# Token pairs 2 and 3 of an SSD scan: B and C in 512-byte rows, turned on VectorE

## Chip, cores and metric

One Trainium2 chip, one core, everything in float32 to the outside. The metric is the device time of one execution in microseconds (us); lower is better. Time before: 355.99 us, the median of three runs (355.82, 355.99, 357.87).

## The reference, cut to what matters

Two blocks follow each other. The first is a Mamba-2 scan in chunks of 32 tokens over x (4 batches, 8 heads, 768 tokens, 32 channels) with B and C (16 states a head) and decays a; the second is a feed-forward block with a learned slope on its negative side.

```python
for c in range(nc):                                   # chunks of 32 tokens
    cum = np.cumsum(la, axis=-1)                      # la: log of the clipped a
    L = np.exp(cum[:, :, :, None] - cum[:, :, None, :]) * causal
    CB = np.einsum('bhin,bhjn->bhij', Cc, Bc)         # contracts over the 16 states
    y_intra = np.einsum('bhij,bhjd->bhid', CB * L, xc)
    y_inter = np.einsum('bhin,bhnd->bhid', Cc, state) * exp(cum)
    state = decay_full * state + sum_j(B_j x_j decay_from_j)   # contracts over tokens
...
h = x @ w_in                                          # 3072 x 256 by 256 x 2048
g = np.maximum(h, 0.0) + alpha * np.minimum(h, 0.0)
out = g @ w_out                                       # 2048 x 256
```

What matters here: B is needed twice, with tokens on the partitions (for the state) and with states on the partitions (for C times B). C is needed with states on the partitions alone. In memory both lie as [batch, head, token, state], so one token of one head is 16 numbers, 64 bytes.

## The kernel before

**Tiling.** The kernel works in chunks of 128 tokens, two chunks (256 tokens) to a "pair", numbered gp = 0 to 11; with 768 tokens a batch has three pairs. Two pairs make a group g of 512 tokens, and the feed-forward block runs by groups. Pairs 0 and 1 are done first by `first_two`, with code of their own. Pairs 2 and 3 run between the feed-forward steps of group 0. From pair 4 on (`fine = gp >= 4`) the stages of `pair` are cut finer and lie between the steps of `quad`, the feed-forward code of groups 1 to 5.

**Order.** There is no scheduler: the order of instructions on each engine is the order of the program, written out by hand. `pair` is a generator; each `ssm(gp)` runs it to its next `yield`. The loop for group 0 goes over f = 4 to 15: `hidden(0, f)` (TensorE, line L1095, then ScalarE L1098 and VectorE L1099), a stage of `ssm(2)` for f up to 10 and of `ssm(3)` from f = 9, the conversion of weight pieces, and `output(f - 4)` (TensorE L1142). So the first stage of pair 2 comes behind `hidden(0, 4)` and that of pair 3 behind `hidden(0, 9)`.

**Weights.** w_in and w_out arrive as 64-bit floats in 16 pieces of 512 KB each, alternating between the two, with rows of 2 KB (`load_weights`, L257, tile `raw`). Each piece is converted by ScalarE (L273, then L283 or L286), VectorE (L296, L308) and GpSimd (L278 clamps, L330 adds); only then can TensorE use it. Below, in4 is the fifth piece of w_in, out1 and out2 the second and third of w_out.

**Loads of a pair.** `load_pair(gp)` issues all on SP's queue. `load_bc(k)` (L192) brings B and C of chunk k into `nat`, tokens on the partitions, in 1024 runs of 64 bytes each; `load_x(k)` (L197) brings x in runs of 128 bytes. For pair 2 `load_pair(2, False, True)` issues chunk 0 only; the two closures it returns are called a little later in `first_two`, between weight pieces. For pair 3 all is issued at f = 5. For pairs above 4 (`turned`), C is not loaded by `load_bc`; instead both B and C are also loaded in four transfers of 128 rows of 512 bytes (L215): 8 tokens of one head lie in one row, even heads and odd heads apart. Transfers of one queue are issued in the order of the program.

**To states on the partitions.** For pairs 2, 3 and 4, `pair` does four TensorE transposes of 128x128 into a PSUM tile (L669) and one ScalarE copy of 128x512 out of it (L672), giving `bc`. For pairs from 5 on, `turn_bc(gp)` does one VectorE instruction (L574) from the 512-byte rows. After that come `spread_c` (ScalarE, L679), `c_decayed` (GpSimd, L682), the C times B products (TensorE, L742), their product with the decays (VectorE, L753) and the products with x (TensorE, L797, L805). `pair_loads` makes `bn` from B with tokens on the partitions (GpSimd, L533); TensorE multiplies it with x at L629. The scans that make the decays are VectorE's, L567 for pairs 2 and 3. `token_sums` is four subtractions on GpSimd (L1183) ahead of the products of a group (TensorE, L1241).

**PSUM.** `ss_tile()` deals tiles in turn from a rotation: two tiles of the pool `ps_s` and one bank of `ps_q`. The transposes of pairs 2 and 3 take one tile each of it.

Of the kernel before, what the change touches and what calls it, by code (L numbers as in the profile page):

```python
# [9 lines left out]
F32 = mybir.dt.float32  # L10
# [12 lines left out]
def kernel(  # L23
# [25 lines left out]
    nc = tc.nc  # L49
# [5 lines left out]
    N = B.shape[-1]  # L55
    P = 128
    Q = 128
# [8 lines left out]
    GC = 4  # L66
# [9 lines left out]
    NB = 2  # L76
# [15 lines left out]
    work = ctx.enter_context(tc.tile_pool(name="work", bufs=2))  # L92
# [4 lines left out]
    gp = ctx.enter_context(tc.tile_pool(name="gp", bufs=16))  # L97
# [15 lines left out]
    def ss_tile():  # L113
        if early[0] is None:
            return ps_s.tile([P, 512], F32, name="ss")
        early[0] += 1
        i = early[0] % (3 if ident_p else 4)
        return ps_s.tile([P, 512], F32, name="ss") if i < 2 else bank(i)


    loads = {}

    def load_rows(i, eng=nc.sync):

        rows = ld.tile([RW, Q], F32, name="rows")
        eng.dma_start(out=rows, in_=a.rearrange("b h (c t) -> (b h c) t", t=Q)[i * RW : (i + 1) * RW])
        loads["r", i] = rows
# [3 lines left out]
    def load_a(t, b, c, eng=nc.sync):  # L131
        first = a[b, 0:1, c * Q : (c + 2) * Q]
        eng.dma_start(out=t, in_=bass.AP(tensor=first.tensor, offset=first.offset,
                                             ap=[[S, H], [0, N], [1, 2 * Q]]))
# [4 lines left out]
    def load_tokens(dst, src, t0):  # L139


        d = dst.rearrange("p j (h w) -> p j h w", h=H)
        for k in range(2):
            for j in range(2):
                t = t0 + k * Q + j * HQ
                nc.sync.dma_start(out=d[HQ * k : HQ * (k + 1), j],
                                  in_=src[:, t : t + HQ, :].rearrange("h p w -> p h w"))

    def load_spread(gp, b, c):

        for w, t in enumerate(loads["p", gp][1] if gp >= HALF else ()):
            rows = scratch["z", b // 2].rearrange("(b h c) t -> b c h t", b=2, h=H)
            for k in range(2):
                nc.sync.dma_start(
                    out=t[HQ * k : HQ * (k + 1), : 4 * SQ].rearrange("p (h t) -> p h t", h=4),
                    in_=rows[b % 2, c + k, 4 * w : 4 * w + 4].unsqueeze(0)
                    .to_broadcast([HQ, 4, SQ]))
        for k, t in enumerate(loads["p", gp][1] if gp < HALF else ()):
            rows = scratch["z", b // 2].rearrange("(b h c) t -> b c h t", b=2, h=H)[b % 2, c + k]
            nc.sync.dma_start(out=t.rearrange("p (h t) -> p h t", h=H),  # L160
                              in_=rows.unsqueeze(0).to_broadcast([P, H, Q]))
            yield

    def load_products(gp, ap):
        b, c = divmod(2 * gp, CPB)
        rows = scratch["pf", b // 2].rearrange("(b h c) t -> b h (c t)", b=2, h=H)
        rows = rows[b % 2, :, c * Q : (c + 2) * Q]
        nc.sync.dma_start(out=ap, in_=rows.unsqueeze(1).to_broadcast([H, N, 2 * Q]))

    def load_pair(gp, decays=True, parted=False):  # L170


        b, c = divmod(2 * gp, CPB)
        turned = gp > GC
        nat = ldx.tile([P, 3, 2, H * N], F32, name="nat")
        xt = ldx.tile([P, 2, HD], F32, name="xt")

        ap = ldx.tile([P, 2 * Q], F32, name="ap")
        if gp == 0:
            load_a(ap, b, c)  # L180
        elif gp > NB:
            load_products(gp, ap)
        if gp == 0:
            load_rows(0, nc.scalar)
        abc = []
        if gp >= HALF:
            load_tokens(nat[:, 0], B[b], c * Q)
        def load_bc(k):
            ts = slice((c + k) * Q, (c + k + 1) * Q)
            for i, src in enumerate((B,) if turned else (B, C)):  # L190
                eng = nc.scalar if gp == 0 and i else nc.sync
                eng.dma_start(out=nat[:, i, k].rearrange("p (h n) -> p h n", h=H),  # L192
                              in_=src[b, :, ts, :].rearrange("h p n -> p h n"))

        def load_x(k):
            ts = slice((c + k) * Q, (c + k + 1) * Q)
            nc.sync.dma_start(out=xt[:, k].rearrange("p (h d) -> p h d", h=H),  # L197
                              in_=x[b, :, ts, :].rearrange("h p d -> p h d"))

        for k in range((1 if parted else 2) if gp < HALF else 0):  # L200
            load_bc(k)
            if gp >= NB:
                load_x(k)
        for k in range(2 if gp < NB else 0):
            load_x(k)
        if gp == 0:
            nc.scalar.dma_start(out=al_n, in_=moe_alpha.rearrange("(k p) -> k p", p=P))
            loads["a", 1] = prep.tile([P, 2 * Q], F32, name="a1")
            load_a(loads["a", 1], b, c + 2)
        for i, src in enumerate((B, C) if turned else ()):  # L210


            for e in range(2):
                first = src[b, e : e + 1, c * Q : (c + 2) * Q, :]
                nc.sync.dma_start(out=nat[:, 1 + e, i],  # L215
                                  in_=bass.AP(tensor=first.tensor, offset=first.offset,
                                              ap=[[2 * S * N, P // 32], [8 * N, 32], [1, 8 * N]]))
        for k in range(2 if gp >= NB else 0):
            abc.append(lda.tile([P, H * Q], F32, name="abc"))
        loads["p", gp] = nat, abc, xt, ap  # L220
        if gp >= HALF:
            load_tokens(xt, x[b], c * Q)
        if decays:
            for part in load_spread(gp, b, c):
                pass
        return lambda: load_bc(1), lambda: load_x(1)
# [6 lines left out]

    al_n = const.tile([NF, P], F32, name="al_n")
    load_pair(0)

    w_in = const.tile([P, KC, d_ff], F32, name="w_in")
# [312 lines left out]
    bcs = {}  # L550
# [3 lines left out]
    def scan_half(dec, abc, k, w):  # L554
        dv = dec.rearrange("p k h t -> p k (h t)")
        if ident_p and halved:
            dv = dec.rearrange("p k h t -> p (k h t)")
            for i in range(2):
                s = (2 * w + i) * SQ
                o = (4 * k + 2 * w + i) * SQ  # L560
                nc.vector.tensor_tensor_scan(out=dv[:, o : o + SQ], data0=abc[k][:, s : s + SQ],  # L561
                                             data1=ident_p[0][:, :SQ], initial=0.0,
                                             op0=ALU.mult, op1=ALU.add)
            return
        for i in range(2):
            hs = slice((2 * w + i) * 2 * Q, (2 * w + i + 1) * 2 * Q)
            nc.vector.tensor_tensor_scan(out=dv[:, k, hs], data0=abc[k][:, hs],  # L567
                                         data1=ident_p[0], initial=0.0, op0=ALU.mult,
                                         op1=ALU.add)

    def turn_bc(gp):

        bcs[gp] = work.tile([P, 4, Q], F32, name="bc")
        nc.vector.transpose(  # L574
            bcs[gp].rearrange("p (i k) t -> p i (k t)", i=2)
            .rearrange("p i (c b) -> p i b c", b=8),
            loads["p", gp][0][:, 1:].rearrange("p e i (b n) -> p (i b) e n", n=N))
        decs[gp] = work.tile([P, 2, H, Q], F32, name="dec")
        scan_half(decs[gp], loads["p", gp][1], 0, 0)

    def pair(gp):

        b, c = divmod(2 * gp, CPB)
        nat, abc, xt, ap = loads["p", gp]
        last = c + 2 == CPB
        fine = gp >= 2 * GC // 2
# [75 lines left out]


        bc = bcs.pop(gp, None)
        if bc is None:
            tp = ss_tile()
            for i in range(2):
                for k in range(2):
                    nc.tensor.transpose(tp[:, (2 * i + k) * P : (2 * i + k + 1) * P],  # L669
                                        nat[:, i, k], ident)  # L670
            bc = work.tile([P, 4, Q], F32, name="bc")
            nc.scalar.copy(out=bc.rearrange("p i t -> p (i t)"), in_=tp)  # L672
# [148 lines left out]
    def first_two():  # L821
# [158 lines left out]
        prq = rows_short(rq)  # L980
        rows_out(0)
        load_pair(1)
        load_second()
        nat1, _, xt1, pf1 = loads["p", 1]
# [420 lines left out]
    def ssm(gp, stages=1):  # L1405

        if gp not in pairs:
            pairs[gp] = pair(gp)
        for i in range(stages):
            next(pairs[gp], None)  # L1410
# [169 lines left out]
```

## Time and profile before

| | us |
|---|---|
| median of three runs | 355.99 |
| span of the profiled execution, first to last instruction | 355.9 |
| TensorE busy (matmul) | 349.3 |
| VectorE, GpSimd, ScalarE busy | 235.8, 204.4, 171.8 |
| share of the DMA engines, 18 to 27, 27 to 36, 36 to 45 us | 0.92, 0.95, 0.96 |
| TensorE clock granted | 1.000 |

For the profiled execution no time beside its span is given; the span lies 0.1 us under the median of the runs, so next to nothing lies around it. Busy time of TensorE counts a matmul from its start to its modelled end; matmuls overlap, so the step from one start to the next is the better measure of what one costs. Names like L1142 are lines of the kernel before; an arrow reads "out <- in". Of the changed kernel, lines from 578 on lie 5 to 7 lower.

### The profile page before, as it was taken

The numbers are of one execution on the slowest core, as the hardware profiler recorded it, in microseconds if no ns is written. First come the engines' busy times: TensorE is split into PE (matmuls) and PEld (weight loads), VectorE is DVE, ScalarE is ACT, GpSimd is POOL, SyncE is SP. The second block draws the span as 40 slices with busy tenths as digits, with TensorE's granted clock in tenths as the row PEclk, the third lists the DMA queues.
The fourth block names the chain that finished last, engine by engine and source line by source line (L and its number), as shares of the span: only waits on it lengthen the run. The fifth ranks groups of instructions, "written<-read, shape, count | busy, mean of one in ns | idle before, by whom it ended". The sixth has DMA issues, their size and how long they took to land.

```text
span 355.9 us, 7778 instructions
## 1 busy us (share of the span) xinstructions
PE 349.3 (98%) x2985; PEld 284.4 (80%) x2985; DVE 235.8 (66%) x482; ACT 171.8 (48%) x391; POOL 204.4 (57%) x228
## 2 busy tenths in 40 slices
PE   8899999999999999999999999999999999999996
PEld 4576665578788888888888888888888888888885
DVE  6876986998748756847747856757856633643363
ACT  3477576535355346345345445345445344443431
POOL 6776568589939855725646626637526535434520
PEclk9999999999999999999999999999999999999999
DMA  7899989607345403503423423422001001001102
GB/s 138 182 202 270 329 174 279 148 17 159 106 83 128 102 3 75 104 2 77 78 57 74 86 51 71 85 55 65 11 2 31 0 2 29 2 1 31 31 0 59
DMA packets 105581, 30.24 MB, mean 85 GB/s; under 512 B 79896, under 2 KB 101448, under 8 KB 105544
## 3 DMA queue, kind: packets, MB, share of 16 engines
q1 hardware_dynamic: 103048, 29.43, 36.3%
q10 hardware_dynamic: 2496, 0.32, 0.6%
q8 instruction: 23, 0.38, 0.5%
q14 instruction: 14, 0.11, 0.1%
HBM read 26.32 MB, written 3.42 MB: 84 GB/s over the span
## 4 chain that ended last, share of the span: by engine, by line
PE 89%; SPq 4%; DMA 3%; DVE 2%; ACT 1%; POOL 1%; issue 0%; DVEq 0%; ACTq 0%
PE bank L1216 33%; PE hp L1241 29%; PE bank L1142 6%; PE ss L1241 6%; PE hp L1095 3%; DMA raw<-in_moe_w_in_dram 2%; SPq L192 2%; PE ss L787 1%; PE ss L731 1%; PE hp L1110 1%; PE bank L1209 1%; PE ss L805 1%; PE ss L779 1%; DMA xt<-in_x_dram 1%; SPq L197 1%; PE ss L742 1%
## 5 line engine op out<-in xcount | busy, mean ns | idle before, releaser
L1298 POOL TENSOR_TENSOR gt<-gt 128x512 f32<-128x512 f32 x58 | 74.2, 1279 | 21.1 <-DVE gt L1226 16.3
L1216 PE MATMUL bank<-gt,w_out 128*128 128x256 f32 x320 | 83.5, 381 | 0.0
L1216 PEld LDWEIGHTS bank<-gt,w_out 128*128 128x128 f32 x320 | 60.1, 190 | 9.2 <-issue 1.0
L1288 POOL TENSOR_TENSOR gt<-gt 128x512 f32<-128x512 f32 x20 | 25.4, 1269 | 62.5 <-DVE gt L1226 49.7
L1226 DVE SCALAR_TENSOR_TENSOR gt<-hp,s_mul,gt 128x256 f32<-128x256 f32 x96 | 42.0, 479 | 29.1 <-ACT gt L1224 26.8
L1224 ACT ACTIVATE gt<-hp,s_alpha 128x256 f32<-128x256 f32 x96 | 40.3, 471 | 34.5 <-PE hp L1241 31.4
L1216 PE MATMUL bank<-gt,ws 128*128 128x256 f32 x224 | 55.9, 379 | 0.0
L1216 PEld LDWEIGHTS bank<-gt,ws 128*128 128x128 f32 x224 | 42.3, 190 | 5.6
L1241 PE MATMUL hp<-xs,w_in 128*128 128x256 f32 x160 | 41.9, 384 | 0.0
L1241 PE MATMUL hp<-xs,ws 128*128 128x256 f32 x160 | 41.1, 380 | 0.0
L1267 DVE TENSOR_TENSOR hp<-hp,u 128x512 f32<-128x512 f32 x20 | 14.0, 700 | 35.2 <-ACT u L1265 35.2
L1241 PEld LDWEIGHTS hp<-xs,ws 128*128 128x128 f32 x160 | 30.3, 190 | 4.3 <-POOL xs L1183 0.2
L1241 PEld LDWEIGHTS hp<-xs,w_in 128*128 128x128 f32 x160 | 29.7, 190 | 4.5
L1142 PE MATMUL bank<-w_out,gt 128*128 128x256 f32 x128 | 31.1, 385 | 0.4 <-POOL w_out L330 0.4
L1142 PEld LDWEIGHTS bank<-w_out,gt 128*128 128x128 f32 x128 | 23.6, 190 | 7.2 <-issue 2.9
L1241 PE MATMUL ss<-xT,w_in 128*128 128x256 f32 x96 | 24.6, 379 | 0.0
L645 POOL TENSOR_TENSOR sm<-state,bmask 128x256 f32<-128x256 f32 (+1 forms) x10 | 6.2, 620 | 29.0 <-DVE state L642 29.0
L1095 PE MATMUL hp<-xT,w_in 128*128 128x512 f32 x48 | 22.8, 596 | 0.0
L561 DVE TENSOR_TENSOR_SCAN dec<-abc,bank 128x192 f32<-128x192 f32 x48 | 22.7, 522 | 0.0
L1256 ACT COPY m<-hp 128x512 f32<-128x512 f32 x8 | 4.7, 586 | 35.7 <-PE hp L1241 35.7
L1265 ACT COPY u<-hp 128x512 f32<-128x512 f32 x20 | 11.7, 585 | 19.4 <-PE hp L1241 19.4
L1226 DVE SCALAR_TENSOR_TENSOR gt<-c,s_mul,gt 128x256 f32<-128x256 f32 x40 | 20.6, 555 | 0.0
(232 smaller groups left out, 608.2 us busy)
## 6 DMA issues: line engine op xcount, KB each, us to landing
abc<-z SPq DMA_DIRECT2D x24, 192.0 KB
raw<-in_moe_w_in_dram SPq DMA_DIRECT2D x8, 512.0 KB
raw<-in_moe_w_out_dram SPq DMA_DIRECT2D x8, 512.0 KB
abc<-z SPq DMA_DIRECT2D x8, 512.0 KB
out_dram<-o_sb SPq DMA_DIRECT2D x32, 64.0 KB
nat<-in_B_dram SPq DMA_DIRECT2D x26, 64.0 KB
xt<-in_x_dram SPq DMA_DIRECT2D x12, 128.0 KB
xt<-in_x_dram SPq DMA_DIRECT2D x24, 64.0 KB
```

The lines of the kernel that those rows point to most:

```text
L192: eng.dma_start(out=nat[:, i, k].rearrange("p (h n) -> p h n", h=H), in_=src[b, :, ts, :].rearrange("h p n -> p h n"))
L561: nc.vector.tensor_tensor_scan(out=dv[:, o : o + SQ], data0=abc[k][:, s : s + SQ], data1=ident_p[0][:, :SQ], initial=0.0, op0=ALU.mult, op ...
L1095: nc.tensor.matmul(hp, w_in[:, k, f * P : (f + 1) * P], xts[g][:, k], start=(k == 0), stop=(k == KC - 1))
L1142: nc.tensor.matmul(pos[0][t // 2][:, t % 2], gt[:, t * Q : (t + 1) * Q], w_out[:, f], start=(f == 0 and t % 2 == 0), stop=(f == NF - 1), s ...
L1216: nc.tensor.matmul(ms[g][i][:, h], w, blocks[g, z][n][:, p], start=(q == 0 and h == 0), stop=(q == NQ - 1), skip_group_check=True)
L1224: nc.scalar.mul(o[:, p], h[:, p], s_alpha[:, fs[p]])
L1226: nc.vector.scalar_tensor_tensor(out=o[:, p], in0=h[:, p], scalar=s_mul[:, fs[p]], in1=o[:, p], op0=ALU.mult, op1=ALU.max)
L1241: nc.tensor.matmul(to[:, p], w(2 * z + p), b, start=start and p == 0, stop=True, skip_group_check=True)
L1265: nc.scalar.copy(out=u2, in_=A)
L1267: nc.vector.tensor_tensor(out=Y, in0=Y, in1=u2, op=ALU.add)
L1288: nc.gpsimd.tensor_tensor(out=tc_, in0=g22, in1=g12, op=ALU.subtract)
L1298: eng.tensor_tensor(out=o, in0=x0, in1=x1, op=ALU.subtract)
```

## The change

Pairs 2 and 3 now also count as `turned`: `load_bc` brings only B for them, and four transfers of 512-byte rows for B and C are added (for pair 2 behind x of chunk 0, for pair 3 behind x of chunk 1). Their four transposes and the copy are gone, and one VectorE instruction stands in their place in the first stage of `pair`. Pair 4 stays as it was.

```diff
@@ load_pair
-        turned = gp > GC
+        turned = gp >= NB and gp != GC        # NB = 2, GC = 4
@@
-    def turn_bc(gp):
-
-        bcs[gp] = work.tile([P, 4, Q], F32, name="bc")
+    def turned_bc(gp):
+
+        bc = work.tile([P, 4, Q], F32, name="bc")
         nc.vector.transpose(
-            bcs[gp].rearrange("p (i k) t -> p i (k t)", i=2)
+            bc.rearrange("p (i k) t -> p i (k t)", i=2)
             .rearrange("p i (c b) -> p i b c", b=8),
             loads["p", gp][0][:, 1:].rearrange("p e i (b n) -> p (i b) e n", n=N))
+        return bc
+
+    def turn_bc(gp):
+
+        bcs[gp] = turned_bc(gp)
         decs[gp] = work.tile([P, 2, H, Q], F32, name="dec")
         scan_half(decs[gp], loads["p", gp][1], 0, 0)
@@ pair
         bc = bcs.pop(gp, None)
+        if bc is None and not fine:
+            bc = turned_bc(gp)
         if bc is None:
             tp = ss_tile()
             for i in range(2):
```

## The prediction

> **What bounds the kernel now.** First the page's sums: TensorE is busy for all but 6.6 us of the span, at full clock, so time can only be won by taking work off TensorE or by ending a wait of it.
>
> ```profile
> PE 349.3 (98%) x2985; PEld 284.4 (80%) x2985; DVE 235.8 (66%) x482; ACT 171.8 (48%) x391; POOL 204.4 (57%) x228
> ```
>
> Then who TensorE waited for (engine, line, releaser: us in total, times, longest). Two of its six rows concern us: L895 waits for x of pair 1, and L1142 for a converted piece of w_out, out2. After that no wait is listed.
>
> ```profile
> PE ss L895 <- DMA xt<-in_x_dram: 0.2, 1, 0.2
> ...
> PE bank L1142 <- POOL w_out L330: 0.4, 1, 0.4
> ```
>
> Then the chain of work that ended last, from 17 to 52 us (start, length, what). It leaves TensorE at 27.4 us and comes back at 45.84; between, it is in4's landing, its conversion, and a queue of VectorE work.
>
> ```profile
> 29.84 7.45 DMA raw<-in_moe_w_in_dram
> ...
> 38.13 0.83 POOL wt L278
> ...
> 38.98 0.69 DVE wr L308
> ...
> 40.34 2.33 DVE dec L567 x4
> ...
> 44.52 1.28 POOL w_out L330
> ...
> 45.84 1.99 PE bank L1142 x8
> ```
>
> Last, the timelines of VectorE and GpSimd (start, length, idle time before it). I followed them back from TensorE's 79.35 us, where its weight load waits 0.2 us for `xs` (L1183, ends 79.28). GpSimd works there from 75.26 on; that start waited for VectorE's L308 at 74.42, which goes back over GpSimd to VectorE's L1099 at 68.25. That one waited 0.27 us for TensorE. VectorE had then been busy from 56.84 on, which goes back over GpSimd to VectorE's L308 at 49.38, and from there nearly without idle time to 38.98.
>
> ```profile
> 35.74 2.41 DVE L567 TENSOR_TENSOR_SCAN dec<-abc,bank 128x256 f32<-128x256 f32 x4
> 38.08 0.40 DVE L296 TENSOR_SCALAR wr<-raw 128x512 uint32<-128x512 uint32 x1
> 38.98 0.69 DVE L308 SCALAR_TENSOR_TENSOR wr<-wt,wr 128x512 uint32<-128x512 uint32 x1 [0.50 <-POOL wt L278]
> ...
> 56.84 0.69 DVE L308 SCALAR_TENSOR_TENSOR wr<-wt,wr 128x512 uint32<-128x512 uint32 x1 [3.08 <-POOL wt L278]
> ...
> 68.25 0.75 DVE L1099 SCALAR_TENSOR_TENSOR gt<-hp,s_mul,gt 128x512 f32<-128x512 f32 x1 [0.27 <-ACT gt L1098]
> ```
>
> So from 39 to 79 us a second chain, VectorE and GpSimd in turn, runs beside a full TensorE with 0.27 us to spare. Both have to become shorter.
>
> **TensorE's part.** Per pair four transposes (L669) go. Start to start they cost 29.46 - 29.02 = 0.44 us for pair 2 and 51.59 - 51.09 = 0.50 for pair 3, together 0.94.
>
> ```profile
> 29.02 0.60 PE L669 MATMUL ss<-ident,nat 128*128 128x128 f32 x4
> 29.46 1.89 PE L1142 MATMUL bank<-w_out,gt 128*128 128x256 f32 x8
> ```
>
> The first 0.44 is won ahead of the wait at 45.84, so it only makes that wait 0.88 instead of 0.44, unless out2 is ready sooner too.
>
> **ScalarE's part.** Two copies (L672, 0.58 us each) go. Worth nothing: behind the first, ScalarE then idles 1.71 us for out1, behind the second 1.26 for TensorE's L1095.
>
> **VectorE's part.** One instruction for each pair is added; pairs from 5 on show the same one (L574) at 1.11 us, all seven within 1.108 to 1.120. Pair 2's comes behind L1099, which ends at 31.34; the next instruction, L296, starts at 32.51 because it waits for out1 to land (1.17 us idle). 31.34 + 1.11 = 32.45: free, with 0.06 to spare. Were out1 sooner, up to 1.11 would be owed, but GpSimd's clamp (1.05 us idle before L308 at 33.99) covers most again. Pair 3's starts at 50.98 and pushes L296 and L308; L308 then ends near 53.6 instead of 52.97, and GpSimd takes its result at 54.84. Free, with 1.2 us to spare; behind it are another 3.08 idle at 56.84. Without that cover it would cost 1.11.
>
> ```profile
> L574 DVE STREAM_TRANSPOSE bc<-nat x7: 1108/1112/1120, 93.5 to 258.2; 128x512 f32<-128x512 f32 x7
> ```
>
> The Trainium skill, "VectorE: DVE Perf Modes", Rules for kernel authors, speaks against the change: it sends a 128x128 transpose to TensorE where a PSUM destination will do, and keeps VectorE's for 32x32 blocks. By that rule, with VectorE taken as the bound, two times 1.11 us would be lost; by the rows above it finds VectorE idle both times.
>
> **The queue and the DMA engines.** This decides. In the trace's packet records a packet of 64 bytes takes 11 ns, one of 512 bytes 27 ns, on one of 16 engines. A transfer of 64 KB is thus 1024 x 11 / 16 = 0.70 us of all engines in short rows, 128 x 27 / 16 = 0.22 in long ones. Each pair loses two of the former (C) and gains four of the latter: 0.88 - 1.40 = -0.52 us. On SP's queue it is the other way: two issues of 0.58 go and four of 0.55 (L215, B 0.57 and C 0.54) come, +1.04 us a pair.
>
> Which of the two counts? Between 15 and 33 us the engines are full (share 0.98 from 22 to 33 us, with a hole of 0.35 from 21 to 22), and five of SP's issues take 1.6 to 2.9 us instead of some 0.5, which I read as a queue that cannot hand over more. SP has thus some 7.6 us of slack there, and the DMA engines none, so I let the 0.52 count. Pair 2's four new issues stand ahead of out0; I expect that piece 0.2 to 1.8 us later (0.88 - 0.70 = 0.18 of transfers; with three more issues at 0.55 on top, if none of them falls into time that SP waits anyway). TensorE uses out0 at 29.46 and GpSimd has it ready at 28.64, so 0.4 us is free once the transposes are gone, and more would eat into a wait that comes anyway at 45.84. Behind it one transfer of short rows is gone, so in3, out1 and in4 come 0.5 sooner.
>
> For pair 3 the issues lie behind in4, out2 and the four pieces after them. They only have to land by 51 us. In before x of chunk 1 is issued at 47.14; two issues of C stand ahead of it, one held for 3.89 us and one of 0.58, and both go, while four of 0.55 come behind it. I expect the long rows to be there by 50.
>
> **The sum.** Call s the time by which VectorE's L308 at 38.98 starts earlier. TensorE at 45.84 moves by s (it could by 0.88), after pair 3 by s + 0.50; the second chain moves by s at first and, as VectorE's 0.27 us of waiting at 68.25 goes, by s + 0.27. TensorE then waits for `xs` at 79.35, so the whole gain is s + 0.27, not s + 0.94. From there to the end TensorE has no listed wait and all follows.
> For s: in4 0.52 sooner would let L308 go at 38.48, where L296 ends, so 0.50 is the cap unless out1 also moves VectorE's scans ahead of it. If instead SP's 1.04 us counted in full, s = -1.04. Nearer to the evidence is the first; I take s = 0.4, less a little for out0. Gain 0.67 on a span of 355.9: 355.2. The span lies 0.1 us under the median of the runs, so I forecast 355.3 us.
>
> **The rivals.**
> - *The long rows arrive, SP becomes the queue that decides* (slower). Place: SP between 16 and 33 us. For it: a held issue leaves the engines empty behind it (share 0.35 from 21 to 22 us), and four small transfers refill them slowly. Against it: the share of 0.98 after that. Price: s = -1.04 gives 355.99 + 1.04 - 0.27 = 356.8; with one more issue held like out0's (1.63) 358.4. It decides as soon as in4 lands more than 0.27 us later than its 37.28.
> - *The loads move more than their packets.* If out1 and in4 both come over 1 us sooner, VectorE's scans start sooner too, and TensorE's own path is the limit: 0.94 + 0.44 = 1.38, so 354.6. For it: five held issues that could dissolve. Against: from 27 to 45 us the engines' share is 0.95 and 0.96, with weights and decays that the change leaves as they are.
> - *Pair 3's rows come late.* VectorE would wait at 50.98 with the conversions of in6 and out4 behind it, and GpSimd for those. From 52.2 us on each us costs one, up to 3: 355.3 + 1 to 3, so 356.3 to 358.3. For it: they are issued last, behind B and x. Against: C's two issues, 3.89 and 0.58 us, no longer stand ahead of them.
>
> **How the numbers follow.** Forecast 0.52, SP 0.29, more than the packets 0.12, late rows 0.07. The forecast's own range is s from 0 to 0.7, 355.7 to 355.0. The range reaches to 354.2 (the third case with a little more) and to 357.6 (the second with one half of the held issue). A measurement here can tell about 1%, 3.6 us. Only a gain beyond all TensorE work removed would be over that: 0.03. A loss over that asks for two held issues more, or two cases together: 0.07. Within 1%: 0.90.
>
> **What the changed profile would show.** L669 left with four matmuls instead of twelve, and L672 with one copy instead of three. L574 nine times at 1.11 us, the two new ones at about 31 and 50.5 us with no idle time for a DMA before the second. in4's conversion (L273 at 37.37) at about 36.9; the wait at L1142 between 0.4 and 0.9 us; TensorE's load waiting some 0.2 us more for `xs` near 79. Packets of 64 bytes 4096 fewer. If in4's conversion starts later than 37.6, or the wait at L1142 is over 1.2 us, the forecast is wrong and the first rival holds; if a DMA wait stands before the second L574, the last one.

## The result, and the profile after

The changed kernel takes 358.05 us (median of 13 runs, 357.27 to 359.03), the kernel before 356.39 on the same chip (13 runs, 355.69 to 357.87). The ratio is 1.0044, with a 95% interval of 1.0030 to 1.0058: the change costs 0.44%, some 1.6 us. The forecast was 355.3, and 358.05 lies above its range too.

Everything that the change is, happened. This is the page of the kernel after, its sums by engine and its line of packets, and the groups of the two lines of the turn (L574 on VectorE; the TensorE transposes, L669 before, are L676 now):

```profile
PE 348.6 (98%) x2977; PEld 283.6 (80%) x2977; DVE 237.4 (67%) x484; ACT 171.3 (48%) x389; POOL 204.3 (57%) x228
...
DMA packets 102477, 30.50 MB, mean 86 GB/s; under 512 B 75768, under 2 KB 98344, under 8 KB 102440
```

```profile
L574 DVE STREAM_TRANSPOSE bc<-nat x9: 1108/1112/1128, 32.1 to 258.3; 128x512 f32<-128x512 f32 x9
L676 PE MATMUL ss<-ident,nat x4: 272/273/327, 78.0 to 78.4; 128*128 128x128 f32 x4
```

TensorE lost 0.7 us of busy time, VectorE got two more instructions of 1.11, and there are 4128 packets under 512 bytes fewer than the 79896 of before. So the loss is in waits. Who TensorE waited for, after (us in total, times, longest):

```profile
PE bank L1149 <- POOL w_out L330: 1.2, 1, 1.2
PE hp L1102 <- DVE gt L1106: 1.0, 1, 1.0
```

Both were short before: 0.4 us for w_out, and no listed wait at L1102. The first also stands elsewhere. Before, it was out2 at 45.84 us; now it is w_out's first piece (out0), at 29.43 us. The chain that ended last shows both places (start, length, what):

```profile
16.57 2.08 SPq L215
...
20.43 5.37 DMA raw<-in_moe_w_out_dram
...
29.43 1.99 PE bank L1149 x8
...
58.44 2.33 DVE dec L567 x4
```

A chain that began, in this stretch, with TensorE's own work now begins with SP, which is held at pair 2's first long transfer (L215) for 2.08 us; then it goes over out0. On VectorE's timeline (start, length, idle time before it) both waits are seen again:

```profile
22.21 0.69 DVE L308 SCALAR_TENSOR_TENSOR wr<-wt,wr 128x512 uint32<-128x512 uint32 x1
...
25.83 0.43 DVE L296 TENSOR_SCALAR wr<-raw 128x512 uint32<-128x512 uint32 x1 [1.09 <-DMA raw<-in_moe_w_out_dram]
...
32.07 1.12 DVE L574 STREAM_TRANSPOSE bc<-nat 128x512 f32<-128x512 f32 x1
...
38.32 0.69 DVE L308 SCALAR_TENSOR_TENSOR wr<-wt,wr 128x512 uint32<-128x512 uint32 x1
...
48.71 0.69 DVE L308 SCALAR_TENSOR_TENSOR wr<-wt,wr 128x512 uint32<-128x512 uint32 x1
...
51.44 1.13 DVE L574 STREAM_TRANSPOSE bc<-nat 128x512 f32<-128x512 f32 x1 [1.03 <-DMA nat<-in_C_dram]
...
56.89 0.69 DVE L308 SCALAR_TENSOR_TENSOR wr<-wt,wr 128x512 uint32<-128x512 uint32 x1 [1.86 <-POOL wt L278]
```

The turn of pair 3 stands still for 1.03 us until the long rows of C have landed, and everything behind it on VectorE with it: the next L296 starts at 52.41 and ends at 52.83. GpSimd's first sum of weights (L1178) then starts at 52.96, after 0.71 us of idle time:

```profile
52.96 1.79 POOL L1178 TENSOR_TENSOR ws<-w_in 128x512 f32<-128x512 f32 x1 [0.71 <-ACT wg L286]
```

By the code `ws` takes the buffer of a `raw` that is read by ScalarE's L286 and by that L296. The profile names ScalarE, which was done at 52.60; L296 is the later of the two, so I read this as a wait for VectorE.

**A ruler for all runs.** VectorE's L308 runs once for each weight piece, and twice for the first, in halves. Four of these starts cut every profile into the same stretches: the 4th (22.21 us in the profile after), the 8th (38.32), the 11th (48.71) and the 13th (56.89). From the 13th to the end all sixteen profiled executions of this study take 298.96 to 299.11 us. From the 8th to the 11th they take 10.38 to 10.48, except one with 10.89. So what differs lies in three stretches: up to the 4th, 4th to 8th (where out0 is waited for) and 11th to 13th (where pair 3's rows are).

| profiled execution | 4th at | 4th to 8th | 11th to 13th | out0's conversion (ScalarE L273) | span |
|---|---|---|---|---|---|
| before, the one the prediction used | 22.91 | 16.07 | 7.47 | 24.67 | 355.9 |
| before, another (`e0_before`) | 22.18 | 15.18 | 7.47 | 24.11 | 354.4 |
| after | 22.21 | 16.11 | 8.18 | 25.83 | 355.9 |

The first column varies from 22.14 to 23.36 from one execution to the next, whatever the kernel, and so does part of the second: 0.9 us between two executions of the kernel before. Single spans are therefore no measure here, and all verdicts below rest on medians and ratios; the stretches tell where to look.

### The profile page after: what moved, and what is told of

Its sections match the earlier page's. It is cut to its first block, busy times and chain, and to the rows that moved or that the text cites. A ratio compares the mean times of both kernels' runs of the same rounds, so it can differ in the third digit from the quotient of the medians.

```text
span 355.9 us, 7764 instructions
## 1 busy us (share of the span) xinstructions
PE 348.6 (98%) x2977; PEld 283.6 (80%) x2977; DVE 237.4 (67%) x484; ACT 171.3 (48%) x389; POOL 204.3 (57%) x228
## 3 DMA queue, kind: packets, MB, share of 16 engines
HBM read 26.58 MB, written 3.42 MB: 84 GB/s over the span
## 4 chain that ended last, share of the span: by engine, by line
PE 88%; SPq 4%; DVE 3%; DMA 2%; POOL 1%; ACT 1%; issue 1%; DVEq 0%; POOLq 0%
PE bank L1223 33%; PE hp L1248 29%; PE bank L1149 6%; PE ss L1248 6%; PE hp L1102 4%; SPq L192 2%; DMA raw<-in_moe_w_out_dram 2%; PE ss L794 1%; DVE dec L567 1%; PE ss L738 1%; PE hp L338 1%; SPq L215 1%; PE bank L1216 1%; PE ss L786 1%; PE ss L812 1%
## 5 line engine op out<-in xcount | busy, mean ns | idle before, releaser
L1149 PE MATMUL bank<-w_out,gt 128*128 128x256 f32 x128 | 31.3, 386 | 1.2 <-POOL w_out L330 1.2
L1149 PEld LDWEIGHTS bank<-w_out,gt 128*128 128x128 f32 x128 | 23.6, 190 | 9.0 <-POOL w_out L330 3.1
L1102 PE MATMUL hp<-xT,w_in 128*128 128x512 f32 x48 | 22.7, 595 | 1.0 <-DVE gt L1106 1.0
```

Source lines behind the costliest of these rows:

```text
L1102: nc.tensor.matmul(hp, w_in[:, k, f * P : (f + 1) * P], xts[g][:, k], start=(k == 0), stop=(k == KC - 1))
L1149: nc.tensor.matmul(pos[0][t // 2][:, t % 2], gt[:, t * Q : (t + 1) * Q], w_out[:, f], start=(f == 0 and t % 2 == 0), stop=(f == NF - 1), s ...
```

## The experiments

The theories, as the expectations name them. A: pair 2's four issues make out0 late. B: pair 3's rows come late, and VectorE waits with the conversions behind. C: VectorE's own time for the turns. D: the long transfers run on 4 of the 16 DMA engines, so they take longer than their bytes. E: it is SP's additional issues, or their bytes, that count.

**Which half of the change, and which part.** Four kernels of one comparison, in which the kernel before has a median of 356.34. Pair 2 alone and pair 3 alone:

```diff
-        turned = gp >= NB and gp != GC
+        turned = gp == NB or gp > GC          # e1_pair2
+        turned = gp > NB and gp != GC         # e2_pair3
...
-        if bc is None and not fine:
+        if bc is None and gp == NB:           # e1_pair2; NB + 1 in e2_pair3
```

> Pair 2 alone as in the change; pair 3 as before. Theory A (pair 2's four issues make out0 late, TensorE waits for it at its first use): 1.0 to 1.6 us slower than before, with a wait of TensorE of about 1.2 us for w_out near 29 us. Theory B (pair 3's long rows land late, VectorE waits for them with the weight conversion queued behind it): within 0.5 us of before. Theory C (VectorE's own 1.1 us a pair falls on a chain of VectorE and GpSimd that has no slack): 0.3 to 1.1 us slower.

> Pair 3 alone as in the change; pair 2 as before. Theory A: 0.5 us faster to no change (the transposes of pair 3 gone). Theory B: 1.0 to 1.7 us slower, with VectorE waiting about 1 us for the long rows ahead of the turn of pair 3, and GpSimd's first weight sum held behind it. Theory C: 0.3 to 1.1 us slower without such a wait.

The loads alone, where the TensorE transposes of before stay and nobody reads the long rows; and the turn alone, with the loads of before, where VectorE turns the rows that were loaded for the transposes (so `bc` holds other numbers, at the same price):

```diff
-        if bc is None and not fine:
+        if False:                             # e3_loads
```
```diff
-        turned = gp >= NB and gp != GC
+        turned = gp > GC                      # e4_turn
...
-            loads["p", gp][0][:, 1:]...
+            loads["p", gp][0][:, (1 if gp > GC else 0):(3 if gp > GC else 2)]...
```

> The loads of the change for both pairs, but the four TensorE transposes and ScalarE's copy of before stay, and VectorE turns nothing for pairs 2 and 3 (the transposes read the first two parts of the tile, so what stands for C there is long rows of B). Theory A: 1.0 to 1.6 us slower than before, out0 late as in the change. Theory B: within 0.5 us of before, since nothing that lies ahead of weight conversions waits for the long rows; TensorE itself may wait for them for up to 0.5 us. Theory C: 0 to 0.5 us faster.

> The loads of before for both pairs, but VectorE turns what lies there (rows of B and C with tokens on the partitions) in place of the TensorE transposes and the copy: one instruction of 128x512 a pair at the same place as in the change, on other data. Theory A: 0.3 to 0.9 us faster. Theory B: 0.2 to 0.7 us faster, no wait for a DMA ahead of the turn of pair 3. Theory C: 0.5 to 2.2 us slower.

| kernel | median | ratio [95%] | 4th to 8th | 11th to 13th | out0's conversion |
|---|---|---|---|---|---|
| e1_pair2 | 356.79 | 1.0011 [0.9997, 1.0026] | 15.45 | 7.47 | 25.19 |
| e2_pair3 | 356.57 | 1.0013 [0.9994, 1.0032] | 14.35 | 8.15 | 23.67 |
| e3_loads | 357.18 | 1.0023 [1.0010, 1.0036] | 15.71 | 7.46 | 26.60 |
| e4_turn | 355.69 | 0.9982 [0.9969, 0.9995] | 14.73 | 7.41 | 23.67 |

The turn on VectorE wins 0.18%, so C falls; the loads alone lose 0.23%, 0.8 us, somewhat less than A had said. The two halves, 0.11 and 0.13%, cannot be told from the kernel before: 0.4 and 0.5 us, where A and B had each said 1.0 us or more, and TensorE's wait for out0 with pair 2 alone is 0.5 us and not 1.2. But each half has its own mark in the profile: out0 late where pair 2's long rows are loaded, a longer 11th to 13th where pair 3's are turned. Where nobody turns the late rows (e3) that stretch stays at 7.46. VectorE's timeline with pair 3 alone has the same wait as the full change:

```profile
50.11 1.13 DVE L574 STREAM_TRANSPOSE bc<-nat 128x512 f32<-128x512 f32 x1 [1.02 <-DMA nat<-in_C_dram]
```

Loads and turn together cost 0.44%, and not 0.23 - 0.18 = 0.05. Part of that is this wait, which neither of them alone can have: 8.18 - 7.46 = 0.72 us, 0.20%.

**The base.** The kernel before was run once more for its profile.

> The kernel before, profiled once more. If its first profile (span 355.9 us) was a long execution, as the 1.7 us between time and span of every other profiled run suggests, its span now lies at 354.5 to 354.9 us, and TensorE reaches the first hidden products at 13.6 to 13.9 us instead of 14.1. If the first profile was typical: 355.7 to 356.1.

It took 356.13 us with a span of 354.4. So 1.7 us lie around the span, as in the profile after (357.59 and 355.9). In this execution TensorE waits for no piece of w_out, and the chain that ended last stays on TensorE from 13.87 us on (followed to 110 us). A part of it (start, length, what):

```profile
28.63 0.44 PE ss L669 x4
29.07 1.73 PE bank L1142 x8
...
42.85 1.72 PE hp L1095 x4
44.56 1.73 PE bank L1142 x8
46.29 1.72 PE hp L1095 x4
```

The way over in4 and VectorE from 27.4 to 45.84 us, and the wait at its end, are not there.

**Each place by itself.** First pair 3's rows ahead of its B and x (theory B), then pair 2's rows behind out1 (A), then pair 3's turn behind two conversions (L296, L308, L296), so that it waits for nothing (B, with the loads as they are):

```diff
+        if gp == NB + 1:                      # e5_rows3_first
+            load_long()                       # the four transfers of L215
         for k in range((1 if parted else 2) if gp < HALF else 0):
             load_bc(k)
...
         load_x()                              # e6_rows2_late, in first_two
         load_next()                           # issues out1
+        load_long()
...
-                if f >= 9:                    # e8_turn3_later
+                if f >= 10:
                     ssm(3)
...
                     convert_a(*pieces[int(i)])
+                    if f == 9:
+                        sign(*pieces[int(i)])
+                        ssm(3)
```

> As the change, but pair 3's four transfers of long rows are issued ahead of its B and x. Theory B (VectorE's wait for them holds the weight conversion): the 1.0 us wait ahead of VectorE's turn of pair 3 is gone, and the time is 0.6 to 0.9 us under the change's, so 0.15 to 0.3% over before. Theory A (out0's lateness through pair 2's issues is the loss): within 0.2 us of the change, 0.4% over before.

> As the change, but pair 2's four transfers of long rows are issued behind out1 and not ahead of out0. Theory A: TensorE's wait of 1.2 us for w_out near 29 us is gone or under 0.3 us, and the time is 0.6 to 1.2 us under the change's, so 0.1 to 0.3% over before. Theory B: the wait is gone, but the time stays within 0.3 us of the change's, since the chain of VectorE and GpSimd, not TensorE, sets the time when pair 3 is through.

> As the change, but VectorE's turn of pair 3 comes behind the next two sign passes (L296) and one L308, in the 3 us in which it waits for GpSimd anyway; loads as in the change. Theory B: the rows are there by then, GpSimd's weight sum is not held, and from VectorE's L308 near 49 us to the one near 57 us it takes 7.4 to 7.5 us as before instead of 8.2; the time is 0.6 to 0.9 us under the change's, 0.15 to 0.3% over before. Theory A: within 0.2 us of the change, 0.4% over before.

| kernel | median | ratio [95%] | 4th to 8th | 11th to 13th | out0's conversion |
|---|---|---|---|---|---|
| e5_rows3_first | 357.52 | 1.0026 [0.9996, 1.0056] | 16.61 | 7.41 | 26.58 |
| e6_rows2_late | 357.44 | 1.0033 [1.0015, 1.0052] | 15.12 | 8.09 | 24.85 |
| e8_turn3_later | 357.40 | 1.0030 [1.0017, 1.0043] | 16.66 | 7.48 | 26.37 |

Each repair takes away its own mark and leaves the other. By the ratios each wins 0.1 to 0.2% of the 0.44, and none all of it; but the three intervals overlap with that of the change, so no single repair is shown to win time. (The kernel before has a median of 356.13 in this comparison, 356.58 in the next.) Both together should:

> As the change, but pair 2's long rows are issued behind out1 and pair 3's ahead of its B and x. Theories A and B together (out0's lateness and VectorE's wait make up the loss, 0.7 us and some 0.9 us): both waits gone, 1.2 to 2.0 us under the change, ratio to before 0.9985 to 1.001. Theory D adds that pair 2's rows hold four of the engines ahead of the decays and in4, so some of it comes back as a later in4: up to 0.5 us. If neither place is the cause: ratio 1.003 to 1.005.

356.57 us, ratio 0.9991 [0.9975, 1.0006], with 15.12 and 7.42 for the two stretches and out0 at 23.70. The loss is gone, with an interval that lies below that of the change. Its timeline of VectorE (lines lie 5 to 7 lower than in the kernel after) has the turn right behind L1112, with no wait:

```profile
49.26 1.12 DVE L579 STREAM_TRANSPOSE bc<-nat 128x512 f32<-128x512 f32 x1
...
55.08 0.69 DVE L313 SCALAR_TENSOR_TENSOR wr<-wt,wr 128x512 uint32<-128x512 uint32 x1 [1.87 <-POOL wt L283]
```

Pair 3 alone with its rows first, which leaves out pair 2's trouble altogether:

> Pair 3 alone as in the change, its long rows issued ahead of its B and x; pair 2 as before. Theory B: the wait of VectorE that pair 3 alone had (1.0 us) is gone, 0.7 us are won over pair 3 alone, so 0.2 to 0.7 us under before, ratio 0.998 to 0.9995. If the wait was not the cost: ratio 1.000 to 1.002 as pair 3 alone.

356.23 us, ratio 0.9993 [0.9979, 1.0008], 15.23 and 7.42. Neither of the two can be told from the kernel before; the wins that are left are smaller than what these runs resolve.

**Why the rows are late: how many engines.** The DMA engines' busy share and rate in the kernel after, 45.5 to 50 us, in 40 slices of 0.11 us; pair 3's long rows begin to move at 45.7:

```profile
DMA  9531110223222223222245789999999998522456
GB/s 150 90 79 32 41 36 5 82 82 91 82 87 77 82 86 91 86 87 82 64 137 164 232 259 310 300 319 328 319 332 346 337 337 255 164 68 91 146 168 182
```

From the 8th to the 19th slice the share is about a quarter and the rate 77 to 91 GB/s: four of sixteen engines, for which 4 x 512 bytes in 27 ns would be 76 GB/s. Behind that the decays' transfers follow and all engines are busy. The Trainium skill, "DMA: Bandwidth & Descriptors", Why a DMA increments its semaphore by 16 and not by 1, has the reason: a transfer uses the largest number of engines, up to 16, that divides the outermost dimension on both sides. Here the source's outermost dimension is the 4 heads of one parity. Two kernels change that for pairs 2 and 3. One has the 32 token blocks outermost, so that the rows come to other partitions than the turn expects, at the same size:

```diff
-              ap=[[2 * S * N, P // 32], [8 * N, 32], [1, 8 * N]]
+              ap=[[8 * N, 32], [2 * S * N, P // 32], [1, 8 * N]]     # e9_spread
```

> As the change, but the rows of the long transfers of pairs 2 and 3 are taken in another order, token blocks outermost (32) and not heads (4): the same bytes, packets and issues; each row lands on another partition than it should, so what is computed is not the reference's. Theory D (a long transfer with heads outermost runs on 4 of the 16 DMA engines, 128 x 27 / 4 = 0.86 us each instead of 0.22; the trace of before shows at most 6 to 7 packets of 512 bytes in flight in such a stretch, 3.6 on average, where other transfers have 20 and more): spread over 16, w_out's first piece is converted by ScalarE from 23.7 to 24.7 us on (25.2 to 26.6 with the change), no DMA wait of VectorE ahead of the turn of pair 3, 7.4 to 7.5 us between VectorE's two L308, and the time is 0.3 to 0.9 us under before, ratio 0.9975 to 0.9992. Theory E (SP's additional issues and the additional bytes delay what is behind them): as the change, ratio 1.003 to 1.005.

The other has eight transfers of 32 partitions for each pair, one for each head, where the token blocks come outermost by themselves:

```diff
-            for e in range(2):
+            for r in range(4 if gp < GC else 0):                       # e10_eight
+                first = src[b, 2 * r : 2 * r + 1, c * Q : (c + 2) * Q, :]
+                nc.sync.dma_start(out=nat[32 * r : 32 * r + 32, 1:, i],
+                                  in_=bass.AP(..., ap=[[8 * N, 32], [S * N, 2], [1, 8 * N]]))
```

> As the change with the right rows, but for pairs 2 and 3 eight transfers of 32 partitions and both head parities (32 KB each) in place of four of 128 partitions. Theory D: they spread over 16 engines as in e9; SP has 4 issues more a pair, 2.2 us at 0.55, of which some falls into time that it waits anyway: 0.6 us under before to 0.5 us over it, ratio 0.998 to 1.0015, no DMA wait ahead of the turn of pair 3 over 0.5 us. Theory E: slower than the change, ratio 1.005 to 1.009.

e9 took 357.67, ratio 1.0035 [1.0017, 1.0053]; e10 took 359.08, ratio 1.0076 [1.0054, 1.0099]. In e9 the same stretch of time, 45.5 to 50 us, has no plateau at a quarter:

```profile
DMA  0348999996443155520145510446402212377899
GB/s 1 50 79 133 176 205 216 165 170 147 133 132 100 55 155 164 150 78 23 55 127 155 173 50 27 109 137 205 119 23 91 68 32 59 91 223 241 255 300 273
```

Pair 3's turn waits for nothing there (51.29 us, 11th to 13th 7.42). D therefore explains the second cost. It doesn't explain the first, or not most of it: out0's conversion starts at 26.81 in e9, as late as ever, and with eight issues at 27.08. E10 moves the same bytes in as many packets as e9, and its four more issues a pair cost 0.4% more (six runs; pair 3's stretch is 7.44, so the loss is not there). So there it goes by the count of issues, which is E.

**Why out0 is late: places on the queue, or bytes.** Two kernels were to separate them. One is the kernel before with four additional transfers of 8 KB ahead of out0, together as many packets as the change's four (512), at an eighth of the bytes. The other is the arrangement of e7 for pair 3, and for pair 2 the four transfers at their early time, but issued by ScalarE, behind its last conversion of in2, the third piece of w_in (the "third study" in the expectation is the comparison that held e7):

```diff
+        if gp == NB:                          # f2_four_small, in load_pair of before
+            few = prep.tile([P, 4, N], F32, name="few")
+            for h in range(4):
+                nc.sync.dma_start(out=few[:, h], in_=B[b, h, c * Q : (c + 1) * Q, :])
...
                 convert_a(*pieces[2])         # f1_act_queue, in first_two
                 sign(*pieces[2])
             if (i, k) == (0, 1):
+                load_long(nc.scalar)
```

> The kernel before, with four additional transfers of 8 KB each (128 rows of 64 bytes) on SP's queue where the change has pair 2's long rows; nothing reads them. Only places on the queue are added, and an eighth of the bytes of the change's four. If out0 is late because of the places on SP's queue: ScalarE's conversion of out0 starts at 25.0 to 26.5 us as in the kernel with pair 2 alone, and the ratio is 1.001 to 1.0035. If it is late because of what the long transfers occupy on the DMA engines: out0's conversion stays at about 24.1 and the ratio is 0.999 to 1.001.

> The change with pair 3's long rows first, as in the third study, and with pair 2's four long transfers issued from ScalarE's queue, between ScalarE's last conversion of in2 and its copies of token pair 1, and so not on SP's queue ahead of out0. If out0 is late because of the places that four issues take on SP's queue: ScalarE's conversion of out0 starts at 23.7 to 24.7 us, VectorE waits for no DMA before its second turn, and the ratio is 0.997 to 0.9995, the turns' own gain of 0.18% showing. If out0 is late because the long transfers occupy the DMA engines ahead of it, whoever issues them: out0's conversion starts at 25 to 26.5 and the ratio is 1.001 to 1.003. The price of the edit itself is four issues on ScalarE, beside its conversions and copies.

f2: 357.62 us against 356.46, ratio 1.0039 [1.0017, 1.0061], a little more than was expected of the places. Four places on the queue, with 32 KB behind them, cost nearly what the whole change costs. SP's timeline in f2:

```profile
17.55 2.86 SPq L197 DMA_DIRECT2D xt<-in_x_dram  x1
20.46 2.00 SPq L213 DMA_DIRECT2D few<-in_B_dram  x4
22.51 0.43 SPq L261 DMA_DIRECT2D raw<-in_moe_w_out_dram  x1
```

and in the other profile of before:

```profile
16.93 2.27 SPq L197 DMA_DIRECT2D xt<-in_x_dram  x1
19.24 0.96 SPq L257 DMA_DIRECT2D raw<-in_moe_w_out_dram  x1
```

In f2 SP is held once, for 2.86 us, and after that it pays 0.43 to 0.58 for every issue, of whatever size; in this profile of before it is held at x, and again for some 0.5 us at out0 itself. Little of these two us of issues falls into the time in which SP waits anyway. They stand behind it, and out0's conversion moves from 24.11 to 27.14. (The profiled execution of f2 was the slowest of its twelve, 359.9 us, so its stretches overstate its median.)

All profiles agree on the count. From the start of in2's issue to that of out0's SP takes 3.4 to 4.0 us where the loads of before lie between them (both profiles of before, e2, e4, e11), 5.0 to 5.9 with four long transfers on four engines (after, e1, e3, e5, e8), 6.5 in e9 and 6.6 in f2, 7.7 with the eight of e10, and 1.6 where none of them lies there (e6, e7, f1).

f1 took 358.18 us (median of the eleven runs that its ratio takes), ratio 1.0057 [1.0028, 1.0086], above both ranges, and out0's conversion stood at 25.88, which by its expectation speaks for the DMA engines. The marker was badly chosen. Out0 itself is early: SP issues it at 16.87 and its packets of 2 KB have all moved by 22.44 us, against 22.70 in the other profile of before and 26.57 in f2. ScalarE is late, since it now pays for the issues:

```profile
19.78 0.68 ACT L278 ACTIVATE wt<-raw 128x512 f32<-128x512 f32 x1 [0.83 <-DMA raw<-in_moe_w_in_dram]
19.79 1.13 ACTq L204 DMA_DIRECT2D nat<-in_B_dram  x1
...
21.13 0.56 ACTq L204 DMA_DIRECT2D nat<-in_B_dram  x1
22.80 1.63 ACTq L204 DMA_DIRECT2D nat<-in_C_dram  x2
24.53 0.27 ACT L961 COPY xT<-ss 128x128 f32<-128x128 f32 x1 [3.50 <-DMA nat<-in_B_dram]
...
25.88 0.71 ACT L278 ACTIVATE wt<-raw 128x512 f32<-128x512 f32 x1
```

The copies of L961 start at 24.53, where they start at 22.52 in the other profile of before, and TensorE waits 1.8 us for them. So the issues cost on ScalarE's queue too.

Whether the bytes hold up out0, f1 does not tell: its long rows begin to move at 22.09 us only, when out0's packets are nearly through. In the profile after they move from 19.5 to 24.0 us, and out0's from 21.6 to 25.1 beside them. From the start of out0's issue to its conversion, which waits for it there, it takes 5.1 to 5.8 us in the five profiles with long rows on four engines ahead, and 4.2 to 4.6 in e9, e10 and f2. So the four engines seem to add about 1 us to out0's way, beside the issues. That this costs time is not shown: e9, which spreads these rows, has no lower ratio than e5 and e8, which leave them as they are (1.0035 against 1.0026 and 1.0030, all three without the wait of pair 3).

In seven of f1's twelve runs the granted clock was 0.990 to 0.995. The five at 0.999 and above have a median of 357.28, 1.0023 of 356.46; why this kernel met a lower clock so often stays open.

No version that turns the right rows beats the kernel before; e4, which is faster, turns others.

## Why the prediction was wrong, step by step

**The turn's side of the sum held.** TensorE's transposes were won and VectorE's time was hidden: e4 is 0.18% of 356.34 faster, 0.64 us, with an interval of 0.2 to 1.1. That this is near the forecast gain of 0.67 is luck. The 0.67 was s + 0.27 with s = 0.4 from the loads, and e4 has the loads of before; by the sum it was to win 0.27, which the interval holds as well. In one profile each, 0.45 of it lies between the 4th and the 8th L308 (15.18 to 14.73), the size of pair 2's 0.44, but two profiles of before differ by more there. That also decides the rule that was weighed there against this trace: sent to VectorE, these two transposes cost nothing.

**"So I let the 0.52 count" is the step that failed.** It set the bytes of a pair, -0.52 us on the DMA engines, against SP's issues, +1.04, and took SP's to vanish in the time that SP is held. f2 adds issues nearly without bytes and loses 0.39%; e10 adds them at the same bytes and loses 0.4% against e9; e9 spreads the bytes and out0 is as late as with the change; f1 takes the issues off SP, and out0 is there at 22.44. SP is held at x or at the first long transfer; the issues that follow cost their 0.5 us each in full. The s of the sum was to be +0.4; its L308 at 38.98 is the 8th, which stands at 37.36 in the other profile of before and at 38.32 after. Over the profiles, the stretch from the 4th to the 8th averages 16.10 in the six with four long transfers on SP ahead of out0 (after, e1, e3, e5, e8, e9) and 15.11 in the seven with neither those nor additional ones (both of before, e2, e4, e6, e7, e11). Between them lies 1.0 us, near the 1.04 that the first rival took for the place; single profiles of one kernel differ by as much.

**"More would eat into a wait that comes anyway at 45.84" failed with it.** Out0's lateness of up to 1.8 us was reckoned, and set against 0.4 of slack and that wait. The wait does not come in the other profile of before, where no wait of TensorE is listed after 22 us; there what out0 is late falls on TensorE at its first use, and the 1.2 us at 29.43 in the profile after are such a wait.

**"128 x 27 / 16 = 0.22" for a long transfer divides by the wrong number.** Four engines carry it: 128 x 27 / 4 = 0.86 us, and the plateau above shows 64 KB at 85 GB/s, 0.77. Four of them take over 3 us where 0.88 was reckoned (42.1 to 45.5 us for pair 3 in e7, where they move ahead of its other loads). "I expect the long rows to be there by 50" failed with it: they were there at 51.4, though SP issued the last of them at 45.99, 1.15 us sooner than x of chunk 1 before. From the plateau alone they would have come near 49; that the decays' transfers, issued right behind, share the four engines from 47.7 on is what the shares suggest, but no run took them away.

**"Free, with 1.2 us to spare" looked at the wrong reader.** It followed VectorE's L308 to GpSimd's L330 at 54.84 (before). The nearer one is L1178 (L1171 before), which stands ahead of that sum on GpSimd and needs the first L296 behind the turn. GpSimd was ready for it at 52.25 in the profile after (51.61 + 0.64), and L296 ended at 52.83: 0.7 us with the handing over, and 0.72 is what the stretch grew by. So a wait of 1.03 us had some 0.3 to spare. The turn's own 1.11 us are free, as was said (e4, e7: 7.41 and 7.42). e8, where L296 goes ahead of the turn, has no wait on GpSimd there and 7.48. The mark named for the case, a DMA wait ahead of the second L574, is what the profile shows; the rival had 0.07.

**Two rivals held at once.** The first (SP) and the third (late rows) have places of their own; e5, e6 and e8 take one away, e7 both. The prediction spoke of two cases together only for a loss above 1%. Its prices, 356.8 and 356.3 against the forecast's 355.3, are 1.5 and 1.0 us; the stretches have 1.0 and 0.7.

**The marks were partly the wrong ones.** In4's conversion was to start later than 37.6 if the first rival held. It started at 35.82, sooner than 37.37 but just as in the other profile of before; out0, ahead of it, was the one that came late. The wait at L1142 (L1149 now) came out at the edge, 1.2 us, but at out0 and no longer at out2.

**The base was off.** "The span lies 0.1 us under the median of the runs" was read as nothing lying around it. 1.7 us lie around the span of every execution here that has a time beside it, so the profiled one was, by estimate, of about 357.6 us, 1.2 over the median. Its 4th to 8th stretch, 16.07, was already as long as with the change. Rows of an execution that already held such a delay, by chance, were taken for the usual ones, and with them a chain that leaves TensorE for 18 us, which that of the other profile of before does not.

How the 0.44% divides between the two places is known only roughly: the intervals reach 0.13 to 0.3% to each side, as far as the parts themselves. That the halves cost 0.11 and 0.13% and the whole 0.44 is within that, and stays unexplained beyond it.

## What to carry to other kernels

Count a transfer in three currencies: bytes, packets and issues; where a queue is held and then issues at a fixed price, four small issues ahead of a critical transfer put it back by about four times that price, even if they carry fewer bytes. Ahead of any duration that is divided by 16, look at the outermost dimension of both sides: a plateau of the engines' share at a quarter tells that four engines carry it. And compare the span with its own execution's time ahead of using it as a base, by a second profile if one can be had: here two executions of one kernel differed by as much as the effect.

## What was not expected of the hardware

- In the profiles after and of f2 an issue that is held (2.08 and 2.86 us, on SP around 17 us) is followed by issues at 0.43 to 0.58 us, whether a transfer has 8 KB (0.43), 64 KB in long rows (0.54) or 512 KB (0.43 to 0.48). In the two of before the next large one, out0's, was held too (1.63 and 0.96).
- Issued by ScalarE, the four long transfers took 1.13, 0.56 and twice 0.8 us of it, and its next computing instruction started right behind the last of them (24.43 and 24.53).
- Two executions of the same kernel differed by 0.7 us up to the 4th L308 and by 0.9 us from there to the 8th, and by under 0.01 us over the last 299 us.
